# A's wo loaded and multiplied between two units of block B; the last V in one piece, B's wo straight behind it

## The chip, the core and the metric

The kernel runs on one core of one Trainium2 chip. The metric is the device time of one execution in microseconds (us); three executions of the kernel before took 1935.48, 1935.49 and 1935.57 us, median 1935.49 us. The engines named below are PE (TensorE, matrix products), DVE (VectorE), ACT (ScalarE), POOL (GpSimd) and SP (SyncE, which here only waits and issues DMAs).

## The reference, cut to what matters

Two independent attention blocks, A and B, each decode one token for a batch of 2 with 32 heads of 192 elements against a cache of 8192 positions. The outputs (2 x 1 x 640 each) are put side by side.

```python
q = (x @ wq)                                  # x 2x1x640, wq 640x6144, as 32 heads of 192
scores = einsum("bhqd,bhkd->bhqk", q, k) * (192 ** -0.5)
p = softmax(scores, axis=-1)
o = einsum("bhqk,bhkd->bhqd", p, v)           # k, v: 2x32x8192x192 bf16
return o.reshape(2, 1, 6144) @ wo             # wo 6144x640
```

The K and V caches of the two blocks make up nearly all of the 836.78 MB that the kernel reads.

## The kernel before, in words

A **unit** is a pair of heads of one batch row. Each block has 32 units (UB), so there are 64 (NP): 0 to 31 are A's, 32 to 63 are B's. For each unit a whole K piece and a whole V piece (6144 KB each) are loaded into a buffer in SBUF, `rings`, which has three slots of 7680 KB. In slots counted modulo 3, V of unit u goes into the slot where K of unit u lay, and K of unit u+1 goes into the slot where V of unit u-2 lay. A slot also holds a whole `wq` or `wo` (7680 KB).

What one unit does:
- DVE multiplies K in place by the query, in four quarters (L241). Each quarter releases `mu`.
- PE sums the products in groups with an identity matrix (L370), 12 matmuls a quarter, 48 in all; `su` counts the halves. When a unit's second half is done, its K slot is free.
- PE next places the result of an earlier unit into a bank of PSUM (`put`, L327, which waits for `on` of DVE), then sums the softmax denominators (L379, which waits for `ex` and `vs`), and then multiplies the **previous** unit's probabilities with its V: 4 groups of 16 matmuls (L385). Each group counts in `pv`.
- DVE reduces the scores (L246, L250, L251), POOL takes the maximum over partitions (L191), ACT copies the result of the V product out (`gather`, L286) and only then makes the unit's exponentials (L302), whose end is `ex`.

PE runs its units in a loop with index t: at t it does the scores of unit t and the V product of unit t-1. The loop body stands once in the code (`pe_main`) and is entered twice. The first time it runs t = 0 to 63, and behind it PE multiplies A's heads with A's wo (`rows`, L339, 96 matmuls). The second time it runs t = 64 (V product of unit 63) and t = 65 (the last `put`), and behind it PE multiplies with B's wo.

SP issues the loads in a fixed order: K of u+1, V of u, K of u+2, V of u+1 and so on, each behind its waits. The K load waits until K of unit u has landed (`ks`) and V of u-2 has been used (`pv`); the V load until V of u-1 has landed (`vs`) and K of u has been used (`su`). So at least one transfer is queued while another lands. Behind V of unit 62 come A's wo (L144, waits for V of unit 61 to be used), V of unit 63 in two halves (L150, waits for K of unit 63 to be used), and five pieces of B's wo (L155, 24, 15, 6, 2 and 1 rows), each of which waits in `ca` until PE has multiplied the same piece of A's wo, for it takes that place.

ACT copies the two products with wo out of PSUM (L312) and ACT and SP store them (L162). The output of `rows` lies in the PSUM bank `qps`, which the queries use as well.

Of the kernel before, what the change touches and what calls it, by code (L numbers as in the profile page):

```python
# [10 lines left out]
def build_kernel(nc, blocks, out):  # L11
    NBLK = len(blocks)
    B, Hn, Sk, Dh = blocks[0]["k"].shape
    D = blocks[0]["x"].shape[2]
# [3 lines left out]
    UB = B * PB  # L18
# [14 lines left out]
    PW = 34  # L33
    PG = 16
    PQ = T // 2 // PG
    CUTS = [48]
    PIECES = [24, 15, 6, 2, 1]

    with ExitStack() as es:
# [29 lines left out]
        ops = ps("ops", [128, 512], F32)  # L69
        qps = ps("qps", [128, 512], F32)  # L70
        oall = ps("oall", [128, 2, 512], F32)
        outps = qps
        scflat = scps[:].rearrange("p k n -> p (k n)")
        oflat = oall[:].rearrange("p k n -> p (k n)")

        Z = {n: sem(n) for n in ("held", "wq", "wq0", "wq1", "xs", "k0", "ks", "vs", "vh", "os", "init", "dv", "xp", "xt",
                                 "pr", "qe", "qk", "qtd", "mu", "su", "re", "mx", "ar", "nbd", "ex", "pv", "od", "dd", "on",
                                 "pl", "oa", "ca", "oe", "wa0")}
        vq = [sem(f"vq{i}") for i in range(2)]
        ws = [sem(f"ws{i}") for i in range(len(PIECES))]  # L80

        def hold(eng, name, value):
# [4 lines left out]
            return blocks[blk][name].rearrange("b h s d -> (b h s d)").rearrange("(u f) -> u f", f=RW)  # L87

        def k_slot(eng, t):
            return eng.snap(((t * 2 + 2 - ((t + (NP - 1)) >> 6)) % 3) * SW)  # L90

        def program_sync(eng):
            for blk in range(NBLK):
                w = blocks[blk]["wq"].rearrange("(j c) n -> j (c n)", c=DC)
                for a, e in (((0, N // 4), (N // 4, SW)) if not blk else ((0, SW),)):
                    eng.dma_start(rings[:, blk * SW + a:blk * SW + e], w[:, a:e]).then_inc(Z[f"wq{blk}"], 16)

            def load(name, blk, row, at, sem):
                src = flat(name, blk)
                src = src[row:row + 128, :] if isinstance(row, int) else src[bass.ds(row, 128), :]  # L100
                dst = rings[:, at:at + RW] if isinstance(at, int) else rings[:, bass.ds(at, RW)]
                eng.dma_start(dst, src).then_inc(Z[sem], 16)  # L102

            load("k", 0, 0, 2 * SW, "k0")
            eng.wait_ge(Z["pr"], NQP)
            load("k", 0, 128, 0, "ks")
            eng.wait_ge(Z["pr"], 2 * NQP)
            load("v", 0, 0, SW, "vs")
            eng.wait_ge(Z["su"], 2)

            def next_k(u, row, blk, at, wait_k, wait_p):
                hold(eng, "ks", wait_k)
                hold(eng, "pv", wait_p)
                load("k", blk, row, at, "ks")

            def next_v(u, row, blk, at, wait_v, wait_s):
                hold(eng, "vs", wait_v)
                hold(eng, "su", wait_s)
                load("v", blk, row, at, "vs")

            def step(t, u0, blk_v, blk_k):
                if isinstance(t, int):
                    u = u0
                    next_k(u, (u + 1) % UB * 128, blk_k, ((2 * u + 3) % 3) * SW, 16 * u + 16, PQ * (u + 1))
                    next_v(u, u % UB * 128, blk_v, ((2 * u + 4) % 3) * SW, 16 * u, 2 * u + 2)
                else:
                    u = eng.snap(t + u0)
                    r = eng.snap((u * 2) % 3)
                    rk, rv = eng.snap(t * 128 + (u0 + 1) % UB * 128), eng.snap(t * 128 + u0 % UB * 128)
                    next_k(u, rk, blk_k, eng.snap(r * SW), eng.snap(u * 16 + 16), eng.snap(u * PQ + PQ))  # L130
                    next_v(u, rv, blk_v, eng.snap(((r + 1) % 3) * SW), eng.snap(u * 16), eng.snap(u * 2 + 2))

            with eng.Fori(0, UB - 2) as t:
                step(t, 1, 0, 0)
            step(0, UB - 1, 0, 1)
            with eng.Fori(0, UB - 1) as t:
                step(t, UB, 1, 1)
            eng.wait_ge(Z["pv"], PQ * NP)
            for blk in range(NBLK):
                w = blocks[blk]["wo"].rearrange("(p r) n -> p (r n)", r=WR)  # L140
                if not blk:
                    r0 = 0
                    for k, n in enumerate(CUTS):
                        eng.dma_start(rings[:, r0 * D:(r0 + n) * D], w[:, r0 * D:(r0 + n) * D]).then_inc(Z[f"wa{k}"], 16)  # L144
                        r0 += n
                    eng.wait_ge(Z["su"], 2 * NP)
                    src = flat("v", 1)[(UB - 1) * 128:UB * 128, :]
                    for g in range(2):
                        a, e = g * RW // 2, (g + 1) * RW // 2
                        eng.dma_start(rings[:, SW + a:SW + e], src[:, a:e]).then_inc(vq[g], 16)  # L150
                else:
                    r0 = 0
                    for k, n in enumerate(PIECES):
                        eng.wait_ge(Z["ca"], k + 1)
                        eng.dma_start(rings[:, r0 * D:(r0 + n) * D], w[:, r0 * D:(r0 + n) * D]).then_inc(ws[k], 16)  # L155
                        r0 += n
            for blk in range(NBLK):
                eng.wait_ge(Z["oe"], blk + 1)
                store(eng, blk, 1)
# [5 lines left out]
        def program_pool(eng):  # L165
# [20 lines left out]
            for blk in range(NBLK):  # L186
                eng.wait_ge(Z[f"wq{blk}"], 32 - 16 * blk)
                eng.sem_inc(Z["wq"], 1)  # L188
            with eng.Fori(0, NP) as t:
                hold(eng, "mx", eng.snap(t + 1))  # L190
                eng.partition_all_reduce(mg[:], mp[:], 128, bass.bass_isa.ReduceOp.max).then_inc(Z["ar"], 1)  # L191
            k = 0
            for i, n in enumerate(CUTS):
                eng.wait_ge(Z[f"wa{i}"], 16)
                while k < len(PIECES) and sum(PIECES[:k + 1]) <= sum(CUTS[:i + 1]):
                    eng.sem_inc(ws[k], 16)
                    k += 1
            eng.wait_ge(vq[0], 16)
            eng.sem_inc(Z["vs"], 16)
            eng.wait_ge(vq[1], 16)  # L200
            eng.sem_inc(Z["vh"], 2)

        def spread(eng, blk):
            eng.wait_ge(Z["pl"], (blk + 1) * UB + 3)
# [6 lines left out]
        def program_vector(eng):  # L211
# [18 lines left out]

            eng.wait_ge(Z["k0"], 16)
            eng.sem_inc(Z["ks"], 16)
            with eng.Fori(0, NP) as t:
                u = eng.snap(t + 1)
                at = k_slot(eng, t)
                q3 = qt[:].unsqueeze(1).broadcast_to([128, TQ, Dh])
# [12 lines left out]
                eng.wait_ge(Z["re"], eng.snap(u * 2))  # L249
                eng.tensor_reduce(mp[0:64, 0:1], sc[0:64, :], AXL.X, ALU.max)  # L250
                eng.tensor_reduce(mp[64:128, 1:2], sc[64:128, :], AXL.X, ALU.max).then_inc(Z["mx"], 1)  # L251
            eng.wait_ge(Z["qtd"], NP + 2)
            spread(eng, 0).then_inc(Z["oa"], 1)
            closing(NP + 1)
            closing(NP + 2)

        def program_scalar(eng):
            eng.sem_inc(Z["qe"], 2)
            eng.sem_inc(Z["ex"], 2)
            eng.sem_inc(Z["od"], 1)  # L260
            eng.sem_inc(Z["qtd"], 1)
            eng.memzero(actd[:, 0:1]).then_inc(Z["xt"], 1)
            eng.wait_ge(Z["xt"], 1)
            eng.activation(actd[:, 1:2], actd[:, 0:1], ACTF.Exp)
# [51 lines left out]
        def program_tensor(eng):  # L316
# [15 lines left out]
            def rows(r0, r1, landed):  # L332
                at = 0
                for k, n in enumerate(PIECES):
                    for r in range(max(at, r0), min(at + n, r1)):
                        if r == at:
                            eng.wait_ge(ws[k], landed)
                        for h in range(2):
                            ins = eng.matmul(outps[32 * h:32 * h + B, 0:NH2], oallS[:, r, :],  # L339
                                             rings[:, r * D + h * NH2:r * D + (h + 1) * NH2],  # L340
                                             start=(r == 0), stop=(r == WR - 1))
                        if r == at + n - 1:
                            ins.then_inc(Z["ca"], 1)
                    at += n
# [7 lines left out]
            with nc.body("pe_main", valid_engines=own):  # L352
                loc = eng.mark_branch_hint_location()
                p = nc.snap(turn, min_val=0, max_val=NBLK - 1)
                late = eng.snap(p * 2)
                with eng.Fori(eng.snap(p * NP), eng.snap(p * 2 + NP)) as t:
                    w = eng.snap(t + 2)
                    with eng.If(t < NP):
                        eng.wait_ge(Z["qtd"], w)
# [12 lines left out]
                    with eng.If(t > 0):  # L372
# [3 lines left out]
                        with eng.If(t < NP + 1):  # L376
                            eng.wait_ge(Z["ex"], w)
                            eng.wait_ge(Z["vs"], eng.snap(t * 16))
                            eng.matmul(ops[0:PW, 448:449], rs[:], ones[:], start=True, stop=True)  # L379
                            v_at = eng.snap(((t * 2 + 2) % 3) * SW)  # L380
                            with eng.Fori(0, PQ) as g:
                                eng.wait_ge(Z["vh"], eng.snap((g & late) + 1))
                                aj, vj = eng.snap(g * (PG * PW)), eng.snap(g * (PG * 2 * Dh) + v_at)
                                for j in range(PG):
                                    ins = eng.matmul(ops[0:PW, 0:2 * Dh], pbflat[:, bass.ds(aj + j * PW, PW)],  # L385
# [1 line left out]
                                                     skip_group_check=True)  # L387
                                ins.then_inc(Z["pv"], 1)
                eng.wait_ge(Z["oa"], eng.snap(p + 1))
                landed = eng.snap(p * 16 + 16)  # L390
                rows(0, 6, landed)
                eng.br("pe_rows")
            with nc.body("pe_first", valid_engines=own):
                eng.sem_inc(Z["pl"], 2)
                eng.sem_inc(Z["pv"], 2 * PQ)
                eng.sem_inc(Z["vh"], 1)
                eng.wait_ge(Z["init"], INIT)
                eng.wait_ge(Z["xs"], 32)
                with eng.Fori(0, DC) as c:
# [81 lines left out]
```

## Time and profile before

| what | number |
|---|---|
| median of the runs | 1935.49 us |
| span of the profiled execution | 1934.3 us |
| bytes read from HBM, over the span | 836.77 MB, 433 GB/s |
| busy: PE, DVE, ACT, POOL | 81%, 56%, 10%, 1% |
| V products, L385, 4096 matmuls | 712.9 us busy |
| sums of K products, L370, 3072 matmuls | 749.0 us busy |
| K products, DVE L241, 256 | 842.5 us busy |

The span runs from the first to the last instruction of the profiled execution; no other time of that execution is given, and the median of the runs is 1.2 us above its span. Shares of busy time are averages over the whole span. Which engine sets the end can only be read at the end, and which sets the pace only in the middle: so the views of single stretches matter more than this table.

### The profile page before, as it was taken

The numbers are of one execution on the slowest core, as the hardware profiler recorded it, in microseconds if no ns is written. First come the engines' busy times: TensorE is split into PE (matmuls) and PEld (weight loads), VectorE is DVE, ScalarE is ACT, GpSimd is POOL, SyncE is SP. The second block draws the span as 40 slices with busy tenths as digits, with TensorE's granted clock in tenths as the row PEclk, the third lists the DMA queues.
The fourth block names the chain that finished last, engine by engine and source line by source line (L and its number), as shares of the span: only waits on it lengthen the run. The fifth ranks groups of instructions, "written<-read, shape, count | busy, mean of one in ns | idle before, by whom it ended". The sixth has DMA issues, their size and how long they took to land.

```text
span 1934.3 us, 31141 instructions
## 1 busy us (share of the span) xinstructions
PE 1558.2 (81%) x7939; PEld 743.0 (38%) x7939; DVE 1075.6 (56%) x717; ACT 186.5 (10%) x598; POOL 27.9 (1%) x83
## 2 busy tenths in 40 slices
PE   5787888887888887888887888887888888888887
PEld 1343333333333333333333333333433333433434
DVE  0665565565565565565565565565565565565560
ACT  2110010010010010010010010010010010010010
POOL 1000000000000000000000000000000000000000
PEclk9899999999999999999999999999999999999999
DMA  9999999999999999999999999999999999999999
GB/s 421 425 439 439 423 439 439 425 437 439 430 432 439 431 431 439 433 429 439 435 427 439 437 425 439 437 425 439 437 425 439 439 425 437 439 430 432 439 435 394
DMA packets 19896, 836.78 MB, mean 433 GB/s; under 512 B 2220, under 2 KB 2360, under 8 KB 2744
## 3 DMA queue, kind: packets, MB, share of 16 engines
q1 hardware_dynamic: 19880, 836.78, 100.0%
q10 hardware_dynamic: 16, 0.01, 0.0%
HBM read 836.77 MB, written 0.01 MB: 433 GB/s over the span
## 4 chain that ended last, share of the span: by engine, by line
DMA 44%; PE 32%; DVE 10%; issue 10%; another core or an unknown queue 2%; DVEq 1%; SPq 0%; ACT 0%; POOLq 0%
DMA rings<-in_B_k_cache_dram 22%; DMA rings<-in_A_k_cache_dram 19%; PE ops L385 18%; PE scps L370 12%; DVE rings L241 10%; DMA rings<-in_A_wo_dram 2%; DMA rings<-in_B_wo_dram 1%; DVEq L241 1%; PE oall L327 0%; PE qps L339 0%; PE ops L379 0%; SPq L102 0%; DVE qrow L212 0%; DVE sc L246 0%
## 5 line engine op out<-in xcount | busy, mean ns | idle before, releaser
L241 DVE TENSOR_TENSOR rings<-rings,qt 128x6144 bf16 x256 | 842.5, 3353 | 722.9 <-DMA rings<-in_B_k_cache_dram 351.0
L385 PE MATMUL ops<-rings,pb 128*34 x4096 | 712.9, 327 | 166.9 <-issue 166.9
L370 PE MATMUL scps<-rings,ident 128*128 x3072 | 749.0, 403 | 105.5 <-DVE rings L241 102.6
L385 PEld LDWEIGHTS ops<-rings,pb 128*34 x4096 | 381.3, 93 | 483.0 <-issue 233.5
L370 PEld LDWEIGHTS scps<-rings,ident 128*128 128x128 bf16 x3072 | 314.5, 102 | 524.0 <-issue 249.6
L246 DVE TENSOR_REDUCE sc<-scps 128x64 f32<-128x1024 f32 x128 | 155.5, 1215 | 81.4 <-PE scps L370 81.4
L286 ACT ACTIVATE oodd<-ops 2x192 f32<-2x192 f32 x65 | 20.9, 321 | 731.4 <-PE ops L385 731.4
L272 ACT ACTIVATE qt<-qps 64x192 bf16<-64x192 f32 x65 | 21.0, 323 | 650.1 <-DVE rings L241 649.6
L302 ACT ACTIVATE pb<-sc,nb 64x128 bf16<-64x128 f32 x128 | 82.4, 644 | 2.6
L322 PE MATMUL qps<-qrow,sel 36*128 (+1 forms) x66 | 21.8, 331 | 72.4 <-issue 69.6
L296 ACT ACTIVATE nb<-mg 64x1 f32<-64x1 f32 x128 | 25.7, 201 | 302.8 <-POOL mg L191 302.1
L191 POOL PARTITION_ALL_REDUCE mg<-mp x64 | 22.7, 354 | 1856.8 <-DVE mp L251 1856.8
L322 PEld LDWEIGHTS qps<-qrow,sel 36*128 (+1 forms) x66 | 6.1, 93 | 94.0 <-issue 94.0
L302 ACT ACTIVATION_READ_ACCUMULATOR pb<-sc,nb 64x1 f32 x128 | 39.2, 306 | 0.0
L411 PE MATMUL scps<-rings,xT 128*4 x120 | 29.4, 410 | 6.3 <-POOLq L188 6.3
L224 DVE RECIPROCAL rc<-ops 2x1 f32<-2x1 f32 x66 | 9.8, 149 | 34.5 <-PE ops L385 34.5
L327 PEld LDWEIGHTS oall<-on,place 2*128 x260 | 12.5, 92 | 29.7 <-issue 29.2
L226 DVE TENSOR_TENSOR oodd<-ops,oodd 2x192 f32<-2x192 f32 x66 | 21.5, 326 | 0.4 <-ACT oodd L286 0.4
L229 DVE TENSOR_SCALAR on<-oodd,rc 2x192 bf16<-2x192 f32 x66 | 20.3, 307 | 2.3
L273 ACT ACTIVATE qt<-qps 64x192 bf16<-64x192 f32 x65 | 21.1, 325 | 0.8
L327 PE MATMUL oall<-on,place 2*128 2x48 bf16 x260 | 19.6, 183 | 1.9 <-DVE on L229 1.7
L411 PEld LDWEIGHTS scps<-rings,xT 128*4 128x4 bf16 x120 | 10.7, 89 | 24.2 <-issue 12.2
(38 smaller groups left out, 109.9 us busy)
## 6 DMA issues: line engine op xcount, KB each, us to landing
rings<-in_A_k_cache_dram SPq DMA_DIRECT2D x32, 6144.0 KB, 26.8
rings<-in_A_v_cache_dram SPq DMA_DIRECT2D x32, 6144.0 KB, 26.5
rings<-in_B_k_cache_dram SPq DMA_DIRECT2D x32, 6144.0 KB, 26.7
rings<-in_B_v_cache_dram SPq DMA_DIRECT2D x31, 6144.0 KB, 26.6
rings<-in_B_wq_dram SPq DMA_DIRECT2D x1, 7680.0 KB, 37.9
rings<-in_A_wo_dram SPq DMA_DIRECT2D x1, 7680.0 KB, 30.7
rings<-in_A_wq_dram SPq DMA_DIRECT2D x1, 7296.0 KB, 20.2
rings<-in_B_v_cache_dram SPq DMA_DIRECT2D x2, 3072.0 KB, 26.8
```

The lines of the kernel that those rows point to most:

```text
L191: eng.partition_all_reduce(mg[:], mp[:], 128, bass.bass_isa.ReduceOp.max).then_inc(Z["ar"], 1)
L226: eng.tensor_tensor(oodd[:], ops[0:2, 0:Dh], oodd[:], ALU.add).then_inc(Z["dd"], 1)
L241: eng.tensor_tensor(k3, k3, q3, ALU.mult).then_inc(Z["mu"], 1)
L246: eng.tensor_reduce(sc[:, h * 2 * TQ:(h + 1) * 2 * TQ], scps[:, 2 * h:2 * h + 2, :].rearrange("p k (t g) -> p (k t) g", g=DG), AXL.X, ALU. ...
L273: eng.activation(qt[64:128, :], qps[64:128, Dh:2 * Dh], ACTF.Identity).then_inc(Z["qtd"], 1)
L296: ins = eng.activation(nb[p0:p0 + 64, :], mg[p0:p0 + 64, h:h + 1], ACTF.Identity, scale=-scale)
L302: ins = eng.activation(pb[p0:p0 + 64, :, h::32], sc[p0:p0 + 64, :].rearrange("p (j a) -> p j a", a=2), ACTF.Exp, bias=nb[p0:p0 + 64, :], s ...
L322: eng.matmul(qps[:, 0:2 * Dh], sel[:].rearrange("p s m -> p (s m)")[:, bass.ds(k, 128)], qrow[:, bass.ds(c, 2 * Dh)], start=True, stop=Tru ...
L327: ins = eng.matmul(oflat[:, bass.ds(sec, WR)], place[:, bass.ds(at - a, 128)], on[:, a * WR:(a + 1) * WR], start=False, stop=False, skip_g ...
L370: ins = eng.matmul(dst, ident[:], src[:, :, 0:DG], start=(j == 0), stop=(j == NJ - 1))
L385: ins = eng.matmul(ops[0:PW, 0:2 * Dh], pbflat[:, bass.ds(aj + j * PW, PW)], rings[:, bass.ds(vj + j * (2 * Dh), 2 * Dh)], start=False, st ...
L411: ins = eng.matmul(scflat[0:4, bass.ds(to + h * QC, QC)], xT[:, c, :], rings[:, bass.ds(at + (c * N + h * QC), QC)], start=(c == 0), stop= ...
```

## The change

A's wo is loaded between two units of block B. A new constant MID = 45 names the place: behind K of unit 46 and V of unit 45, SP issues A's wo into slot 2 (WO), where V of unit 44 lay. From there on every K and V lies one slot further on, which the new terms with TA = 47 in `k_slot` and in the V address say. PE's loop runs t = 0 to 46 on its first entry; behind it come A's rows, and on the second entry t = 47 to 65. DVE copies A's result out (`spread`) behind its unit 44, for which its loop is split in two.

At the end, V of unit 63 is loaded in one piece as soon as V of unit 61 has been used, and B's wo directly behind it into slot 2, with no wait between its pieces. The wait per V group on `vh`, with its two register operations, is gone from the V product. The product with wo now goes to the second bank of `oall` in place of `qps`.

SP's queue at the end of the program before (rows that issue a DMA, with the semaphores that they wait for; `pv` counts V products, `su` K sums, `ca` pieces of A's wo that have been used):

```order
L144 DMA rings<-in_A_wo_dram 128x30720 [waits pv]
L150 DMA rings<-in_B_v_cache_dram 128x12288 [waits su]
L150 DMA rings<-in_B_v_cache_dram 128x12288
L155 DMA rings<-in_B_wo_dram 128x15360 [waits ca]
L155 DMA rings<-in_B_wo_dram 128x9600 [waits ca]
L155 DMA rings<-in_B_wo_dram 128x3840 [waits ca]
L155 DMA rings<-in_B_wo_dram 128x1280 [waits ca]
L155 DMA rings<-in_B_wo_dram 128x640 [waits ca]
```

The same queue of the changed program, from the end of B's first loop on:

```order
L138 COMPARE_AND_BRANCH
L142 DMA rings<-in_A_wo_dram 128x30720 [waits pv]
L103 DMA rings<-in_B_k_cache_dram 128x24576 [waits ks,su]
L103 DMA rings<-in_B_v_cache_dram 128x24576 [waits vs,pv]
L103 DMA rings<-in_B_k_cache_dram 128x24576 [waits ks,ca]
L103 DMA rings<-in_B_v_cache_dram 128x24576 [waits vs,su]
L157 UNCONDITIONAL_BRANCH
```

And its end:

```order
L103 DMA rings<-in_B_v_cache_dram 128x24576 [waits pv]
L164 DMA rings<-in_B_wo_dram 128x15360 [waits su]
L164 DMA rings<-in_B_wo_dram 128x9600
L164 DMA rings<-in_B_wo_dram 128x3840
L164 DMA rings<-in_B_wo_dram 128x1280
L164 DMA rings<-in_B_wo_dram 128x640
```

A's wo has left the place between the last two V loads, and stands ahead of K of unit 47; the next four loads have their K and V waits exchanged, since their slots have moved on by one.

On PE, the start of one group of the V product before (register rows are marked ISA or REGISTER_ALU):

```order
L379 MATMUL ops<-ones,rs 34x1 [waits vs]
L381 UNCONDITIONAL_BRANCH
L381 ISA
L382 REGISTER_ALU x2
L385 ISA [waits vh]
L385 ISA
L385 MATMUL ops<-rings,pb 34x384
```

and the same place of the changed program:

```order
L391 MATMUL ops<-ones,rs 34x1 [waits vs]
L393 UNCONDITIONAL_BRANCH
L393 ISA
L396 ISA x2
L396 MATMUL ops<-rings,pb 34x384
```

Two register operations and a wait have left the loop over the four groups.

```diff
-    CUTS = [48]
+    MID = 45
+    TA = MID + 2
+    WO = 2 * SW
...
-        outps = qps
+        outps = oall[:, 1, :]
...
-            return eng.snap(((t * 2 + 2 - ((t + (NP - 1)) >> 6)) % 3) * SW)
+            return eng.snap(((t * 2 + 2 - ((t + (NP - 1)) >> 6) + ((t + (NP - TA)) >> 6)) % 3) * SW)
...
-            with eng.Fori(0, UB - 1) as t:
-                step(t, UB, 1, 1)
+            with eng.Fori(0, MID + 1 - UB) as t:
+                step(t, UB, 1, 1, 0)
+            eng.wait_ge(Z["pv"], PQ * (MID + 2))
+            eng.dma_start(rings[:, WO:WO + SW], wo[0]).then_inc(Z["wa0"], 16)
+            m = MID + 1
+            hold(eng, "ks", 16 * m + 16)
+            hold(eng, "su", 2 * m + 2)
+            load("k", 1, (m + 1) % UB * 128, ((2 * m + 4) % 3) * SW, "ks")
+            hold(eng, "vs", 16 * m)
+            hold(eng, "pv", PQ * (m + 2))
+            load("v", 1, m % UB * 128, ((2 * m + 5) % 3) * SW, "vs")
+            m = MID + 2
+            hold(eng, "ks", 16 * m + 16)
+            eng.wait_ge(Z["ca"], len(PIECES))
+            load("k", 1, (m + 1) % UB * 128, ((2 * m + 4) % 3) * SW, "ks")
...
+            with eng.Fori(0, NP - 1 - (MID + 3)) as t:
+                step(t, MID + 3, 1, 1, 1)
             eng.wait_ge(Z["pv"], PQ * NP)
...
-                        eng.dma_start(rings[:, r0 * D:(r0 + n) * D], w[:, r0 * D:(r0 + n) * D]).then_inc(Z[f"wa{k}"], 16)
...
-                        eng.dma_start(rings[:, SW + a:SW + e], src[:, a:e]).then_inc(vq[g], 16)
...
-                        eng.wait_ge(Z["ca"], k + 1)
-                        eng.dma_start(rings[:, r0 * D:(r0 + n) * D], w[:, r0 * D:(r0 + n) * D]).then_inc(ws[k], 16)
+            load("v", 1, (UB - 1) * 128, ((2 * NP - 1) % 3) * SW, "vl")
+            eng.wait_ge(Z["su"], 2 * NP)
...
+                eng.dma_start(rings[:, WO + r0 * D:WO + (r0 + n) * D], wo[1][:, r0 * D:(r0 + n) * D]).then_inc(ws[k], 16)
...
-            with eng.Fori(0, NP) as t:
+            def unit(t):
...
-            eng.wait_ge(Z["qtd"], NP + 2)
+            with eng.Fori(0, TA - 2) as t:
+                unit(t)
             spread(eng, 0).then_inc(Z["oa"], 1)
+            with eng.Fori(TA - 2, NP) as t:
+                unit(t)
...
-                late = eng.snap(p * 2)
-                with eng.Fori(eng.snap(p * NP), eng.snap(p * 2 + NP)) as t:
+                with eng.Fori(eng.snap(p * TA), eng.snap(p * (NP + 2 - TA) + TA)) as t:
...
-                            v_at = eng.snap(((t * 2 + 2) % 3) * SW)
+                            v_at = eng.snap(((t * 2 + 2 + ((t + (NP - TA)) >> 6) - (t >> 6)) % 3) * SW)
                             with eng.Fori(0, PQ) as g:
-                                eng.wait_ge(Z["vh"], eng.snap((g & late) + 1))
...
                 eng.wait_ge(Z["oa"], eng.snap(p + 1))
-                landed = eng.snap(p * 16 + 16)
+                eng.wait_ge(Z["wa0"], 16)
+                landed = eng.snap(p * 16 + 1)
                 rows(0, 6, landed)
```

More of the change, by code (lines that the diff above doesn't have):

```diff
@@ L71, in build_kernel @@
         oall = ps("oall", [128, 2, 512], F32)
-        outps = qps
+        outps = oall[:, 1, :]
         scflat = scps[:].rearrange("p k n -> p (k n)")
         oflat = oall[:].rearrange("p k n -> p (k n)")
-        Z = {n: sem(n) for n in ("held", "wq", "wq0", "wq1", "xs", "k0", "ks", "vs", "vh", "os", "init", "dv", "xp", "xt",
+        Z = {n: sem(n) for n in ("held", "wq", "wq0", "wq1", "xs", "k0", "ks", "vs", "vl", "os", "init", "dv", "xp", "xt",
                                  "pr", "qe", "qk", "qtd", "mu", "su", "re", "mx", "ar", "nbd", "ex", "pv", "od", "dd", "on",
                                  "pl", "oa", "ca", "oe", "wa0")}
-        vq = [sem(f"vq{i}") for i in range(2)]
         ws = [sem(f"ws{i}") for i in range(len(PIECES))]
@@ L119, in next_v, with step @@
                 load("v", blk, row, at, "vs")
-            def step(t, u0, blk_v, blk_k):
+            def step(t, u0, blk_v, blk_k, shift):
                 if isinstance(t, int):
                     u = u0
-                    next_k(u, (u + 1) % UB * 128, blk_k, ((2 * u + 3) % 3) * SW, 16 * u + 16, PQ * (u + 1))
-                    next_v(u, u % UB * 128, blk_v, ((2 * u + 4) % 3) * SW, 16 * u, 2 * u + 2)
+                    next_k(u, (u + 1) % UB * 128, blk_k, ((2 * u + 3 + shift) % 3) * SW, 16 * u + 16, PQ * (u + 1))
+                    next_v(u, u % UB * 128, blk_v, ((2 * u + 4 + shift) % 3) * SW, 16 * u, 2 * u + 2)
                 else:
                     u = eng.snap(t + u0)
-                    r = eng.snap((u * 2) % 3)
+                    r = eng.snap((u * 2 + shift) % 3)
                     rk, rv = eng.snap(t * 128 + (u0 + 1) % UB * 128), eng.snap(t * 128 + u0 % UB * 128)
@@ L131, in step @@
                     next_v(u, rv, blk_v, eng.snap(((r + 1) % 3) * SW), eng.snap(u * 16), eng.snap(u * 2 + 2))
+            wo = [blocks[blk]["wo"].rearrange("(p r) n -> p (r n)", r=WR) for blk in range(NBLK)]
             with eng.Fori(0, UB - 2) as t:
-                step(t, 1, 0, 0)
-            step(0, UB - 1, 0, 1)
-            with eng.Fori(0, UB - 1) as t:
-                step(t, UB, 1, 1)
-            eng.wait_ge(Z["pv"], PQ * NP)
[L139 to L153, printed above, removed]
-                        eng.wait_ge(Z["ca"], k + 1)
-                        eng.dma_start(rings[:, r0 * D:(r0 + n) * D], w[:, r0 * D:(r0 + n) * D]).then_inc(ws[k], 16)
-                        r0 += n
@@ new lines, in program_sync @@
+                step(t, 1, 0, 0, 0)
+            step(0, UB - 1, 0, 1, 0)
+            with eng.Fori(0, MID + 1 - UB) as t:
+                step(t, UB, 1, 1, 0)
+            assert (2 * MID + 2) % 3 == 2
+            eng.wait_ge(Z["pv"], PQ * (MID + 2))
[4 more added lines that the diff above has]
+            load("k", 1, (m + 1) % UB * 128, ((2 * m + 4) % 3) * SW, "ks")
@@ new lines, in program_sync @@
+            hold(eng, "vs", 16 * m)
[5 more added lines that the diff above has]
+            load("k", 1, (m + 1) % UB * 128, ((2 * m + 4) % 3) * SW, "ks")
+            hold(eng, "vs", 16 * m)
+            hold(eng, "su", 2 * m + 2)
+            load("v", 1, m % UB * 128, ((2 * m + 5) % 3) * SW, "vs")
+            with eng.Fori(0, NP - 1 - (MID + 3)) as t:
+                step(t, MID + 3, 1, 1, 1)
@@ L157, in program_sync @@
+            eng.wait_ge(Z["pv"], PQ * NP)
+            load("v", 1, (UB - 1) * 128, ((2 * NP - 1) % 3) * SW, "vl")
+            eng.wait_ge(Z["su"], 2 * NP)
+            r0 = 0
+            for k, n in enumerate(PIECES):
+                eng.dma_start(rings[:, WO + r0 * D:WO + (r0 + n) * D], wo[1][:, r0 * D:(r0 + n) * D]).then_inc(ws[k], 16)
+                r0 += n
             for blk in range(NBLK):
@@ L188, in program_pool, with maxima @@
                 eng.sem_inc(Z["wq"], 1)
-            with eng.Fori(0, NP) as t:
[L190 to L198, printed above, removed]
+            def maxima(a, e):
+                with eng.Fori(a, e) as t:
+                    hold(eng, "mx", eng.snap(t + 1))
+                    eng.partition_all_reduce(mg[:], mp[:], 128, bass.bass_isa.ReduceOp.max).then_inc(Z["ar"], 1)
+            for k in range(len(PIECES)):
+                eng.sem_inc(ws[k], 1)
+            maxima(0, NP)
+            eng.wait_ge(Z["vs"], 16 * (NP - 1))
+            eng.wait_ge(Z["vl"], 16)
             eng.sem_inc(Z["vs"], 16)
-            eng.wait_ge(vq[1], 16)
-            eng.sem_inc(Z["vh"], 2)
         def spread(eng, blk):
@@ L232, in program_vector @@
             eng.sem_inc(Z["ks"], 16)
-            with eng.Fori(0, NP) as t:
+            def unit(t):
                 u = eng.snap(t + 1)
@@ L261, in program_scalar @@
             eng.sem_inc(Z["qtd"], 1)
+            eng.sem_inc(Z["pl"], 2)
+            eng.sem_inc(Z["pv"], 2 * PQ)
             eng.memzero(actd[:, 0:1]).then_inc(Z["xt"], 1)
@@ L339, in rows @@
                             ins = eng.matmul(outps[32 * h:32 * h + B, 0:NH2], oallS[:, r, :],
-                                             rings[:, r * D + h * NH2:r * D + (h + 1) * NH2],
+                                             rings[:, WO + r * D + h * NH2:WO + r * D + (h + 1) * NH2],
                                              start=(r == 0), stop=(r == WR - 1))
@@ L393, in program_tensor @@
             with nc.body("pe_first", valid_engines=own):
-                eng.sem_inc(Z["pl"], 2)
-                eng.sem_inc(Z["pv"], 2 * PQ)
-                eng.sem_inc(Z["vh"], 1)
                 eng.wait_ge(Z["init"], INIT)
```

## The prediction

> **What bounds the kernel now.** I start with the page's DMA part and the windows, then SP's waits, then the last 70 us of the timeline. First the page, and the bytes in a long stretch of the middle (columns of a windows row: length; busy time of each engine with its instructions; granted clock; DMA share; GB/s).
>
> ```profile
> span 1934.3 us, 31141 instructions
> q1 hardware_dynamic: 19880, 836.78, 100.0%
> 200.00:1600.00 1400.00, 1136.82 (x5755) 544.21 (x5753) 803.99 (x532) 128.23 (x434) 17.35 (x49) 0.97 1.00 434
> 1866.70:1932.10 65.40, 52.28 (x395) 27.13 (x393) 18.60 (x18) 5.28 (x17) 0.35 (x1) 0.97 0.98 421
> SPq L84 <- DMA rings<-in_B_v_cache_dram: 357.4, 30, 12.0
> SPq L84 <- DMA rings<-in_B_k_cache_dram: 351.8, 31, 11.7
> ```
>
> In the middle the DMA engines are busy all the time at 434 GB/s. The two SP rows say why: after issuing a load, SP waits some 12 us (357.4/30, 351.8/31) for the **earlier** transfer to land. Every load is thus queued about 12 us before its turn, and the queue never runs dry. 836.78 MB at 434 GB/s take 1928 us of the 1934.3: before, transfers set the pace. Now the end, from the timeline (start, length, engine, line, operation, count, idle time before it):
>
> ```profile
> 1838.10 13.17 DVE L241 TENSOR_TENSOR rings<-rings,qt 128x6144 bf16 x4 [10.90 <-DMA rings<-in_B_k_cache_dram]
> 1867.12 13.16 DVE L241 TENSOR_TENSOR rings<-rings,qt 128x6144 bf16 x4 [11.05 <-DMA rings<-in_B_k_cache_dram]
> 1868.53 0.36 SPq L144 DMA_DIRECT2D rings<-in_A_wo_dram  x1
> 1877.64 5.58 PE L370 MATMUL scps<-rings,ident 128*128 x24 [0.95 <-DVE rings L241]
> 1883.25 0.83 SPq L150 DMA_DIRECT2D rings<-in_B_v_cache_dram  x2
> 1884.34 2.81 PE L385 MATMUL ops<-rings,pb 128*34 x16 [0.57 <-issue]
> 1894.79 2.77 PE L385 MATMUL ops<-rings,pb 128*34 x16 [0.71 <-issue]
> 1898.93 0.30 ACT L302 ACTIVATION_READ_ACCUMULATOR pb<-sc,nb 64x1 f32 x1
> 1899.37 6.68 PE L339 MATMUL qps<-rings,oallS 128*2 128x320 bf16 x96 [1.81 <-POOLq L196]
> 1902.83 4.14 SPq L155 DMA_DIRECT2D rings<-in_B_wo_dram  x5
> 1906.91 0.22 PE L379 MATMUL ops<-ones,rs 128*34 128x1 f32 x2
> 1907.75 2.77 PE L385 MATMUL ops<-rings,pb 128*34 x16 [0.62 <-issue]
> 1918.15 2.77 PE L385 MATMUL ops<-rings,pb 128*34 x16 [0.69 <-issue]
> 1923.73 4.69 PEld L339 LDWEIGHTS qps<-rings,oallS 128*2 128x2 bf16 x48 [0.65 <-issue]
> 1932.15 0.08 PEld L339 LDWEIGHTS qps<-rings,oallS 128*2 128x2 bf16 x2 [0.30 <-DMA rings<-in_B_wo_dram]
> ```
>
> The last K (unit 63) lands just ahead of 1867.12. PE's chain from there is: K sums to 1883.22 (DVE's quarters pace it), V product of unit 62 to 1897.56, A's rows, V product of unit 63 to 1920.92, B's rows. A's rows start 0.1 us after A's wo landed, as the chain of waits shows, and the last matmuls wait for B's wo:
>
> ```profile
> 1868.53 30.75 DMA rings<-in_A_wo_dram
> 1905.68 25.22 DMA rings<-in_B_wo_dram
> 1930.95 1.52 PE qps L339 x18
> ```
>
> So the end is a DMA end too. Had B's wo been there, its 96 matmuls, begun at 1923.73, would have been done about 1 us earlier (7.8 us, below, gives 1931.5 against 1930.95 + 1.52 = 1932.47). **PE has about 1 us of slack here**, and only because A's wo (18 us of transfer) stands between the last two V loads. That slack decides this change.
>
> **The transfers.** No byte is added or removed, so the question is whether the queue stays full and what is left to compute once the last K has landed. Two K starts lie 1867.12 - 1838.10 = 29.0 us apart for two loads of 6144 KB, 14.5 us each; A's wo, 7680 KB, takes 14.5 x 7680/6144 = 18.1 us. The bytes between two V loads move ahead of K of unit 47: **the last K lands 18.1 us later**, at about 1885 in the old count.
>
> The middle, counted from DVE's start on K of unit 46 (0) with the old offsets: V 44 is used at 1868.53 - 1867.12 = 1.4, so A's wo is issued there. V 45 lands at 14.1, A's wo at 32.2. K 46 is used at 16.1 (1883.22), so K 47 is issued 16 us ahead of its turn. V 45 is used at 30.4 (1897.56), then V 46 is issued, also 16 us ahead of 46.7, when K 47 lands. A's rows run from about 32.5 to 39.2 (6.68 us); PE would otherwise idle until K 47, so they cost nothing there. Their `ca` frees K 48, which waits for K 47 to land (46.7) anyway; its turn comes at 61.2. The in-order SP holds up nothing with these waits: each is met 12 us or more ahead of an empty queue. Without this cover each microsecond of a dry queue would cost one. The two extra loop entries (DVE, SP, PE) fall into idle times of 11 us (DVE's row above), 12 us and 7 us. I price the middle at 0; below, nothing can be gained by a queue that is already full; above, a late K 48 would have to be 22 us late (61.2 - 39.2) to count.
>
> **The end.** Now V 63 is issued 1.4 after DVE's start on the last K and lands at 14.1 + 14.5 = 28.6, ahead of its use. B's wo follows and lands at 46.7, that is at 1867.12 + 18.1 + 46.7 = 1931.9, as before: the bytes are the same. But PE's chain does not get its 18.1 us back. Step by step, in the old count plus 18.1:
> - V product of unit 62 ends at 1897.56 + 18.1 = 1915.66.
> - Before, A's rows covered ACT's exponentials of unit 63 (done at 1898.93 + 0.30 = 1899.23, 1.67 behind the V product). Now PE waits for them, and needs 0.84 from L379 to the first matmul (1907.75 - 1906.91): 2.55 with the step between. 1918.21.
> - V product of unit 63: 1907.75 to 1920.92, 13.17. 1931.38.
> - Copy, `put` and spread up to B's rows: 1923.73 - 1920.92 = 2.81. 1934.19. B's wo is complete by then.
> - B's rows, all 96 in one go. The rows for their speed (matmuls in brackets, granted clock third from the end):
>
> ```profile
> 1900.00:1902.00 2.00, 2.00 (x34) 1.27 (x31) 0.00 (x0) 0.00 (x0) 0.00 (x0) 1.00 0.91 393
> 1924.00:1926.00 2.00, 2.00 (x18) 0.99 (x16) 0.00 (x0) 0.00 (x0) 0.00 (x0) 0.50 1.07 461
> 1926.00:1928.00 2.00, 2.00 (x26) 1.10 (x22) 0.00 (x0) 0.00 (x0) 0.00 (x0) 0.74 0.85 365
> ```
>
> At the full clock A's 96 took 6.68 us. B's met a clock of 0.50 after the pause ahead of them: their first 48 loads took 4.69, and 48 at 34 in 2 us take 2.8, with 0.3 for the last to end: 7.8. I take 7.8, since the same pause stands there again. Low end 6.68; high end, at 18 in 2 us throughout, 10.7. 1941.99.
> - Copy out and store: 1934.3 - 1932.47 = 1.83. 1943.82.
>
> The V product's loop has lost two register operations and a wait per group. PE's queue at a group's start, 1861.1 to 1862.6 (ns; first and last start):
>
> ```profile
> L381 PEldq COMPARE_BRANCH  x1: 227/227/227, 1861.3 to 1861.3; - x1
> L382 PEldq ALU_OP  x2: 42/42/43, 1861.7 to 1861.8; - x2
> L385 PEldq FUSED_REGOPS  x4: 69/74/178, 1861.9 to 1862.5; - x4
> ```
>
> The two operations start at 1861.7 and 1861.8, the next at 1861.9: 0.1 each with their spacing, in a gap of about 0.7 us where PE waits for its queue. They are worth up to 0.2 a group, 0.3 with the wait, but the V address has more terms now (no row shows their price; the fused row of 178 ns, which the address is part of, is the nearest). I take 0.125 a group; 4 groups in two V products make 1.0 us, ends 0 and 2.4. In the middle this saves nothing, since PE waits there for K.
>
> **Sum:** 1943.82 - 1.0 = 1942.8 of span against 1934.3, that is +8.5 us; on the median, 1.2 above the span, **1944.0 us, +0.44%**. The "ca" waits and the halves of V 63 go at no gain: the five pieces were issued at 1902.83, some 11 us ahead of V 63's landing (1884.8 + 29 = 1913.8), and behind the change V 63 is whole before PE asks for it.
>
> **The clock.** The pause ahead of B's rows is 2.81 us with a `put` in it, and behind it the granted clock was 0.50 (row of 1924). [...]
>
> **The rivals.**
> 1. *No clock drop ahead of B's rows.* Of the pauses shown, that at 1899 (1.81 us) had none. Then rows take 6.68 and the time is 1944.0 - 1.1 = **1942.9 us**. [...]
> 2. *A clock drop in the V product of unit 63 too.* Its pause of 2.55 us is new. From 0.50 at 1924 to 0.74 at 1926 the clock is low for some 3.4 us; at half pace that loses up to 1.7: **1945.7 us**.
> 3. *A's wo slips in partly.* The page's GB/s in 40 slices:
>
> ```profile
> GB/s 421 425 439 439 423 439 439 425 437 439 430 432 439 431 431 439 433 429 439 435 427 439 437 425 439 437 425 439 437 425 439 439 425 437 439 430 432 439 435 394
> ```
>
> The best slices reach 439 against the mean of 434. Were that a queue that is not quite full, a unit would have 0.33 us to spare (29.0 x 5/439), 18 units behind the change 6 us: **1938 us**. The DMA share of 1.00 in the middle speaks against it. (The 394 of the last slice is mostly the 2 us behind the last landing, and not a queue run dry.)
> 4. *The other side: faster.* If most of A's wo went through in transfer time that is idle today, the last K would not move, and B's wo would land at 1931.9 less the same gain: PE's chain from the old K start gives 1942.8 - 18.1 = 1924.7 of span, **1926 us**. It turns faster than before once more than 8.5 of the 18.1 us are hidden in the middle. Against it stands SP's 12 us of waiting for an earlier transfer.
> 5. *The middle runs dry*, by a wait met late (K 48 behind `ca`, say): every microsecond beyond 22 us of cover counts; 5 us would give **1949 us**.
> 6. *The change does not do what it says* (A's wo stays where it was): the order of SP's queue excludes it.
>
> **Chances.** Forecast (one drop, ahead of B's rows) 0.45, rival 1 0.23, rival 2 0.17, rival 3 0.05, rival 4 0.03, rival 5 or a PE end slower still 0.07. The range takes in the first three with their unknown prices: low end 1942.9 with the loop's saving at its 2.4 (another 1.4 off), 1941.5; high end 1945.7 with no saving and somewhat slower rows, 1947.5. A measurement of this kernel can tell some 0.2% (3.9 us) from no change: slower 0.92, same 0.05, faster 0.03.
>
> **What the profile after should show.** A's wo issued in the middle of B; behind it DVE's K starts once 47 us apart and then 29.0 again; GB/s in those slices as ever; DVE's last K start near 1885; V product of unit 63 about 2.5 us behind that of unit 62; B's wo landed near 1932, ahead of the start of B's rows near 1933; no DMA wait in B's rows. The forecast is wrong if the last K starts well ahead of 1885 (transfers were not full), if some gap in the DMA row opens behind A's wo, or if the two V products at the end are much shorter than 13 us.

## The result, and the profile after

The changed kernel took 1947.72 us (median of four runs, 1946.68 to 1948.02) beside 1935.53 us of the kernel before (1935.48 to 1936.09). The ratio is 1.0061, with a 95% interval of 1.0047 to 1.0075: slower by 0.6%. Two later rounds of the same kernel on other occasions gave 1947.41 us (ratio 1.0054, 1.0038 to 1.0071) and 1946.10 us (1.0052, 1.0035 to 1.0068). The forecast was 1944.0 us, 8.5 us more than before, with a range up to 1947.5. The direction and the mechanism hold. The measured change of 12.2 us is larger than the forecast one, and this median lies 0.2 us above the range; the section on the prediction takes the terms apart, one of which varies from run to run.

The page and two windows of the changed kernel:

```profile
span 1946.5 us, 30606 instructions
q1 hardware_dynamic: 19736, 836.77, 99.3%
200.00:1600.00 1400.00, 1131.03 (x5770) 542.42 (x5769) 792.34 (x524) 127.31 (x430) 17.11 (x48) 0.96 1.00 434
1932.00:1934.00 2.00, 0.31 (x3) 0.09 (x1) 0.81 (x3) 0.32 (x1) 0.00 (x0) 1.00 0.01 3
```

The middle, which holds A's wo now, runs at the same 434 GB/s with the DMA engines busy all the time. But at 1932 the transfers are over, 14 us ahead of the end of the span. Before, they ended about 2 us ahead of it (PE's last weight loads of B's rows, which waited for B's wo, start at 1932.15 of 1934.3).

Around the place where A's wo is loaded, the timeline of the changed kernel (start, length, engine, line):

```profile
1374.34 3.36 DVE L249 TENSOR_TENSOR rings<-rings,qt 128x6144 bf16 x1 [10.84 <-DMA rings<-in_B_k_cache_dram]
1375.77 0.36 SPq L142 DMA_DIRECT2D rings<-in_A_wo_dram  x1
1390.55 0.36 SPq L103 DMA_DIRECT2D rings<-in_B_k_cache_dram  x1
1404.86 0.34 SPq L103 DMA_DIRECT2D rings<-in_B_v_cache_dram  x1
1406.61 6.68 PE L352 MATMUL oall<-rings,oallS 128*2 128x320 bf16 x96 [1.86 <-DMA rings<-in_A_wo_dram]
1420.95 0.34 SPq L103 DMA_DIRECT2D rings<-in_B_k_cache_dram  x1
1421.46 6.63 DVE L249 TENSOR_TENSOR rings<-rings,qt 128x6144 bf16 x2 [29.14 <-DMA rings<-in_B_k_cache_dram]
1450.48 3.36 DVE L249 TENSOR_TENSOR rings<-rings,qt 128x6144 bf16 x1 [10.80 <-DMA rings<-in_B_k_cache_dram]
```

Once, two K starts lie 1421.46 - 1374.34 = 47.1 us apart, and the next two 29.0 again: A's wo costs its 18.1 us of transfer and nothing besides. Its 96 matmuls lie at 1406.61, in the idle time of PE ahead of K of unit 47. (Of the four loads behind A's wo only the first two, K of unit 47 and V of unit 46, have their waits exchanged, other than the section on the change says; K of unit 48 waits for A's rows, and V of unit 47 waits as ever.)

The end, from the chain of waits (start, length, what):

```profile
1885.46 3.37 DVE rings L249
1889.51 12.22 PE scps L382 x48
1902.65 2.77 PE ops L396 x16
...
1913.04 2.84 PE ops L396 x16
1915.90 0.33 ACT oodd L299
1916.26 0.36 DVE oodd L234
1916.64 0.32 DVE on L237
1916.95 0.54 issue
1917.50 0.63 PE oall L340 x4
1918.19 0.22 PE ops L391 x2
1918.98 2.79 PE ops L396 x16
...
1929.43 2.79 PE ops L396 x16
1933.90 0.61 PE oall L340 x4
1935.12 9.63 PE oall L352 x96
1944.78 0.43 ACT out_sb L325
```

There is no DMA in it any more from the last K to the end. It is DVE and PE on the last K, the V products of units 62 and 63, and B's rows. Before, the last wait of this chain was for a transfer of B's wo.

### The profile page after: what moved, and what is told of

It reads as the page before. It is cut to its first block, busy times and chain, and to the rows that moved or that the text cites. A ratio compares the mean times of both kernels' runs of the same rounds, so it can differ in the third digit from the quotient of the medians.

```text
span 1946.5 us, 30606 instructions
## 1 busy us (share of the span) xinstructions
PE 1559.7 (80%) x7939; PEld 744.1 (38%) x7939; DVE 1075.6 (55%) x717; ACT 186.8 (10%) x598; POOL 28.0 (1%) x83
## 4 chain that ended last, share of the span: by engine, by line
DMA 42%; PE 36%; DVE 9%; issue 9%; another core or an unknown queue 2%; DVEq 1%; SPq 0%; ACT 0%
DMA rings<-in_B_k_cache_dram 23%; DMA rings<-in_A_k_cache_dram 19%; PE ops L396 19%; PE scps L382 15%; DVE rings L249 9%; DVEq L249 1%; PE oall L352 0%; PE oall L340 0%; PE ops L391 0%; SPq L103 0%; DVE qrow L220 0%; DVE sc L254 0%; DVE oall L224 0%; DVEq L231 0%
```

## The experiments

Times are medians; "span" is the span of the instructions in each run's record. Short diffs are against the changed kernel, or, where it says so, against the kernel before.

**A0, A1. The changed kernel again**, as a yardstick.

> The changed kernel once more, as the yardstick of the runs beside it. Theory 1 (the end is PE's chain behind the last K): 1946.7 to 1948.0 us as before, more spread than the kernel before, because the granted clock in B's rows varies from run to run.

> The changed kernel beside it: spans of 1943.6 to 1946.5 us, as its runs had so far, times of 1945 to 1948 us.

Measured 1947.41 us and 1946.10 us; the eight spans lie between 1943.6 and 1945.3 us. The kernel before, in the same rounds, has spans of 1934.1 to 1934.6 us. The changed kernel spreads more than three times as wide, as theory 1 expects of an end that hangs on PE. One run of A0 took 1945.07 us, below the 1946.7 that were expected at the least.

**E1. A's wo twelve units later.**

```diff
-    MID = 45
+    MID = 57
```

> A's wo 12 units later (behind K of unit 58). Theory 1 (A's wo takes its 18 us of transfer wherever it stands ahead of the last K; the middle costs nothing of its own): as the changed kernel, within 1 us. Rival (the units behind the move are slower, by their new slots and addresses): the loss of 12 us shrinks with the units behind it from 17 to 5, to about 3.6 us, that is 8 us faster than the changed kernel.

Measured 1946.20 us (ratio 1.0054, 1.0037 to 1.0071), beside 1947.41 us for A0. The difference of 1.2 us is 0.2 more than was expected, but within the spread (spans 1943.7 to 1945.5, beside 1943.6 to 1945.3), and far from the 8 us of the rival. In this kernel's profile the V product of unit 62 starts at 1902.71, in that of the changed kernel at 1902.65. Between these two places of A's wo there is no difference; the units behind the move are not slower.

**E2. The kernel before without A's wo load** (A's output is computed from other data).

```diff
-                        eng.dma_start(rings[:, r0 * D:(r0 + n) * D], w[:, r0 * D:(r0 + n) * D]).then_inc(Z[f"wa{k}"], 16)
...
-                eng.wait_ge(Z[f"wa{i}"], 16)
```

> The kernel before without A's wo load: A's rows multiply what lies in the slot, and V of unit 63 is queued directly behind V of unit 62. Theory 1 (A's wo covered PE's work behind the last K): of 18 us of transfer taken away only 1 to 4 us come back, about 2.4 us faster, since PE's chain behind the last K stays. Rival (the end of the kernel before is the end of its transfers and nothing else is near): 14 to 18 us faster.

Measured 1932.03 us beside 1935.73 us (ratio 0.9984, 0.9974 to 0.9993): 3.7 us of the 18 come back. Two windows of this kernel show that the transfers even stand still (second number from the end: DMA share):

```profile
1881.00:1884.00 3.00, 2.71 (x17) 1.15 (x14) 1.82 (x2) 0.06 (x1) 0.00 (x0) 1.00 0.00 0
1899.00:1902.00 3.00, 3.00 (x48) 1.95 (x46) 0.00 (x0) 0.25 (x2) 0.00 (x0) 1.00 0.02 8
```

PE is busy there while the DMA engines wait for it: V of unit 63 for the last K sums and B's wo for A's rows, whose places they take. And in this kernel's chain of waits no transfer stands between the last K and the end. So behind the last K the kernel before was nearly as much bound by PE as by its transfers: A's wo filled time in which PE had work anyway. This is the same mechanism as in the changed kernel, without any of its new code.

**E3. The changed kernel without B's wo load** (B's output is computed from other data).

```diff
-                eng.dma_start(rings[:, WO + r0 * D:WO + (r0 + n) * D], wo[1][:, r0 * D:(r0 + n) * D]).then_inc(ws[k], 16)
...
-                landed = eng.snap(p * 16 + 1)
+                landed = 1
```

> B's wo is not loaded; B's rows multiply what lies in the slot. Theory 1: the end waits for no transfer, so nothing changes, within 1 us of the changed kernel (the clock in B's rows). Rival (the end is still the end of the transfers): 18 us less transfer, up to 18 us faster.

Measured 1946.34 us (ratio 1.0054, 1.0037 to 1.0070), spans 1943.6 to 1945.2, as A0 and A1. Eighteen microseconds of transfer at the very end are worth nothing: the end of the changed kernel waits for no transfer.

**E4. The kernel before without B's wo load**: the same edit there (B's output is computed from other data).

> The kernel before without B's wo load: B's rows multiply what lies in the slot. Theory 1: PE's chain has about 1 us of slack against the last transfer, so the time falls by about 1 us (2 us with a full clock in B's rows; 1 us slower with two low stretches). Rival (the last pieces of B's wo cost the end much more than the chain of PE): 5 us faster or more.

Measured 1935.22 us beside 1935.73 us (ratio 0.9995, 0.9986 to 1.0005). Three of the ten runs took 1933.3 to 1933.5 us, seven 1934.8 to 1935.6: between 2.4 and 0.1 us faster. This fits the length of B's rows: one of the seven was profiled, with rows of 8.04 us and a span of 1933.5, and with 6.68 us in their place (an estimate) the span would be 1932.1, as the three have it (1932.1 to 1932.3). The kernel before has a slack of this size against its last transfer, no more; and since its end waits for that transfer, its time hardly shows how fast B's rows are.

**E5. The kernel before with the last V in one piece.**

```diff
-                    for g in range(2):
-                        a, e = g * RW // 2, (g + 1) * RW // 2
-                        eng.dma_start(rings[:, SW + a:SW + e], src[:, a:e]).then_inc(vq[g], 16)
+                    eng.dma_start(rings[:, SW:SW + RW], src).then_inc(vq[0], 16)
...
-            eng.wait_ge(vq[1], 16)
```

> The kernel before with V of unit 63 in one piece. Theory 1: there, the V product waits for the whole V (landed at about 1913.7 in place of a first half that is there by 1907.7), PE's chain loses its 1 us of slack and more: 5 to 8 us slower. Rival (the halves do not matter): no change.

Measured 1942.13 us beside 1935.73 us (ratio 1.0033, 1.0021 to 1.0044): 6.4 us slower. The timeline of this kernel:

```profile
1913.93 0.27 PE L376 MATMUL ops<-ones,rs 128*34 128x1 f32 x2 [7.07 <-POOLq L197]
1914.75 9.86 PE L382 MATMUL ops<-rings,pb 128*34 x48 [0.54 <-issue]
```

PE stands idle for 7.07 us until the whole V is there. In the changed kernel the whole V is no loss: it is issued at 1886.95 and lands 27.4 us later, at 1914.3, before PE has finished unit 62; PE asks for it only at 1918.2. So of the parts of the change, "the last V whole" is dear where A's wo stands ahead of it, and free where it does not.

**E6, E8. PE's pause ahead of B's rows filled** with matmuls that nobody reads: nine of 36 rows in E6, six of all 128 rows in E8.

```diff
+                        with eng.If(t > NP):
+                            for _ in range(6):
+                                eng.matmul(scps[:, 0, :], ident[:], rings[:, 0:512], start=True, stop=True)
                         eng.wait_ge(Z["on"], w)
```

> Nine matmuls of 128x384 that nobody reads fill PE's pause between the last V product and the last put. Theory (B's 96 matmuls took 9.6 us because the clock was at 0.50 behind the pause): they take 6.7 us, the time falls by some 2 to 3 us. Rival (they are slow because the product goes to another bank of PSUM, or out of another slot): they stay at 9.6 us, and the time stays or rises by up to 1 us.

> As e6, but the matmuls that fill the pause use all 128 rows and columns of the array (six of 128x128 by 512) in place of 36 rows. If what counts for the clock is how much of the array works, the clock stays at 1.00 ahead of B's rows, which take 6.7 us in the profile, and the spans no longer spread over 3 us: all near 1944. If the pause itself (0.9 us ahead of the first of them) is enough, or the clock follows something else, B's rows take 8.0 us or more again in the profile or in some of the spans. The time outside the span, 5.0 us in e6 against 1.5 to 2.6, is looked at too: no theory.

E6 was a miss: 1949.99 us (ratio 1.0070, 1.0053 to 1.0086), with the clock at 0.50 in its profile all the same, and spans from 1944.0 to 1945.8. In E8's profile the clock stands at 1.00, and its four spans are 1944.1 to 1944.2 us. First E6, then E8 (granted clock third from the end, PE's matmuls in the first brackets), then B's rows of E1, which has no filling:

```profile
1936.00:1938.00 2.00, 2.00 (x18) 0.97 (x16) 0.00 (x0) 0.00 (x0) 0.00 (x0) 0.50 0.00 0
```

```profile
1935.58 6.87 PE L352 MATMUL oall<-rings,oallS 128*2 128x320 bf16 x96 [0.53 <-ACT oallS L215]
1936.00:1938.00 2.00, 2.00 (x34) 1.28 (x30) 0.00 (x0) 0.00 (x0) 0.00 (x0) 1.00 0.00 0
```

```profile
1935.19 6.68 PE L352 MATMUL oall<-rings,oallS 128*2 128x320 bf16 x96 [0.66 <-ACT oallS L215]
```

So the clock is what makes B's rows long, and neither the other bank of PSUM nor the other slot: E1's rows use both and take 6.68 us, as A's rows do there in the changed kernel. That the filling kept the clock in E8 is likely, not shown. E1's profile, and E9's below, have the full clock in B's rows without it, and nine of the 24 runs with this end in which no filling was executed (the first four, A0, A1, E1, E3 and E9) have spans of 1943.6 to 1944.3 too; what speaks for the filling is that all four spans of E8 are alike. It is no gain as a change, though: E8 took 1948.98 us (ratio 1.0068, 1.0051 to 1.0085), because 4.7 to 5.0 us of its time lie outside the span, where the changed kernel has 1.5 to 2.6.

**E9. The same matmuls in the program, never executed** (`t > NP + 1`).

> e8's code with a condition that never holds: the six matmuls stand in PE's program and are not executed. e6 and e8 took 4.7 to 5.1 us of device time outside the span of their instructions, the changed kernel 1.5 to 2.6. If that follows from PE's longer program, it is about 5 us here too; if it follows from executing the matmuls, it is 1.5 to 2.6 us, and the time is that of the changed kernel within 1 us.

Measured 1945.50 us (ratio 1.0053, 1.0036 to 1.0069), with 1.5 to 2.3 us outside the span; in its profile B's rows took 6.68 us. So the extra 3 us go with executing them, not with the longer program. Where they lie, no view shows; that stays open.

**E7. The changed kernel with the last K in two halves**, DVE starting on the first.

```diff
-            with eng.Fori(0, NP - 1 - (MID + 3)) as t:
+            with eng.Fori(0, NP - 2 - (MID + 3)) as t:
                 step(t, MID + 3, 1, 1, 1)
...
+            for g in range(2):
+                a, e = g * RW // 2, (g + 1) * RW // 2
+                eng.dma_start(rings[:, WO + a:WO + e], src[:, a:e]).then_inc(Z[f"kh{g}"], 16)
...
+                    if last and q % 2 == 0:
+                        eng.wait_ge(Z[f"kh{q // 2}"], 16)
```

> The changed kernel with K of unit 63 in two halves, DVE starting on the first 7 us earlier; the last unit of DVE's loop stands on its own. Theory 1 (the end is the chain DVE, PE behind the last K): DVE no longer sets the pace of the K sums, PE still has to end unit 61's V product first (1886.9): 1.5 to 3 us faster than the changed kernel. Rival (something else sets the end): no change.

Measured 1945.24 us (ratio 1.0047, 1.0030 to 1.0064), spans 1941.5 to 1943.3, beside 1943.6 to 1946.5 of all runs of the changed kernel. Its profile and that of A0 have B's rows of the same 8.36 us, and spans of 1943.3 and 1945.3: 2.0 us faster, as expected. The timeline of E7:

```profile
1878.14 6.63 DVE L261 TENSOR_TENSOR rings<-rings,qt 128x6144 bf16<-128x6144 bf16 x2 [3.56 <-DMA rings<-in_B_k_cache_dram]
1885.39 6.63 DVE L261 TENSOR_TENSOR rings<-rings,qt 128x6144 bf16<-128x6144 bf16 x2 [0.62 <-DMA rings<-in_B_k_cache_dram]
1888.96 12.21 PE L395 MATMUL scps<-rings,ident 128*128 x48 [0.63 <-DVE rings L261]
1901.38 5.51 PE L409 MATMUL ops<-rings,pb 128*34 x32
```

DVE is done 6.6 us earlier (1892.0), but PE starts its K sums only 0.55 us earlier, at 1888.96 against 1889.51, since it still has unit 61's V product ahead of it. The sums then take as long as before, 12.21 us against 12.22, though DVE was expected to hold them up no longer. The other 1.4 us come behind them: the first two groups of unit 62's V product follow at once and without a gap (1901.38, 32 matmuls), where the changed kernel begins at 1902.65 and pauses 0.68 us between them. In the changed kernel PE's queue works out the first addresses of these groups from 1902.2 on, 0.5 us behind the end of the sums (1901.73); in E7 PE had them in time for the first load at 1901.35. Why the queue was earlier is not shown; that DVE's products were done so early fits it. So a shorter chain ahead of the end does shorten the time, but the size was met in part by luck.

No version that computes both outputs beat the kernel before. That none of this kind can is argued, not shown: in those whose windows show it (the first run, A0, A1, E6 and E8) the bytes land near 1932, with a DMA share of 0.69 to 0.72 from 1930 to 1932 and of 0.00 to 0.01 in the next 2 us, and the kernel before ends about 2 us later.

## Why the prediction was right, point by point

1. *The queue stays full in the middle; A's wo costs 18.1 us there and nothing else.* Shown: 47.1 us between two K starts, 434 GB/s, and E1. The last K started at 1885.46, against 1867.12 + 18.1 = 1885.2.
2. *The end turns from a DMA end into a PE end.* Shown by the chain of waits, by E3 (no transfer is waited for) and by E2 (PE's work behind the last K was nearly binding before). The rivals in which A's wo slips into idle transfer time (3 and 4) and that of a dry queue (5) are out. Rivals 1 and 2 are about the clock; see below.
3. *The sum was short by 3.7 us of span* (1946.5 against 1942.8). Step by step: last K + 0.2; the loop's saving that did not come + 1.0; the step to the V product of unit 63 + 0.55; B's rows 9.63 in place of 7.8, + 1.8; the rest under 0.1. On top, the time outside the span, which I took as 1.2 us, was 1.5 us in the profiled execution and up to 2.4 in the other three. That the result lies near the top of the range is luck in part: of the range's 3.5 us above the forecast, 1.7 were the price of rival 2, which cost nothing, and the step to unit 63's V product, which did cost, was not in them.

The mis-sized term that counts is **B's rows**. I took one low stretch of the clock, as the profile of before showed, and put a longer one (10.7 us for the rows, at 18 matmuls in 2 us throughout) outside what I summed. Four profiles with this end have 6.68 us (E1), 8.02 (A1), 8.36 (A0) and 9.62 (the first run), and span less rows is 1937.0, 1936.9, 1936.9 and 1936.9. In these four profiles all spread is thus this one term; the other runs of these kernels have no profile. Other things can vary too: in E9's profile the rows took 6.68 us and the span less rows is 1937.6, since its chain is late already ahead of them: the last group of unit 63's V product starts at 1930.14, in the others at 1929.39 to 1929.49. In the first run, the windows show 0.50 twice in a row:

```profile
1934.00:1936.00 2.00, 1.37 (x12) 0.77 (x13) 0.00 (x0) 0.28 (x1) 0.00 (x0) 0.58 0.00 0
1936.00:1938.00 2.00, 2.00 (x18) 0.94 (x16) 0.00 (x0) 0.00 (x0) 0.00 (x0) 0.50 0.00 0
1938.00:1940.00 2.00, 2.00 (x18) 1.05 (x16) 0.00 (x0) 0.00 (x0) 0.00 (x0) 0.50 0.00 0
1940.00:1942.00 2.00, 2.00 (x26) 1.07 (x24) 0.00 (x0) 0.00 (x0) 0.00 (x0) 0.72 0.00 0
1942.00:1944.00 2.00, 2.00 (x34) 1.30 (x30) 0.00 (x0) 0.00 (x0) 0.00 (x0) 1.00 0.00 0
```

At 0.50 in the low stretch and 1.00 outside it, these rows make a low stretch of some 6.8 us (1.7 + 2 + 2 + 1.1), an estimate; the rows of A0 (0.90, 0.50 and 0.75 from 1934 to 1940) make 3.4. So the same pause ahead of the same rows was followed by no low stretch (E1, rows of 6.68 us), by one of some 3.4 us (A0, 8.36 us), or by one of some 6.8 us (the first run, 9.62 us). What sets its length is not shown.

So rival 1, no clock drop ahead of B's rows, came true in E1 and, by their spans, likely in A0's and A1's shortest runs; at 1943.6 to 1943.7 their spans still lie 1.9 us above the rival's 1941.7 (1942.9 less 1.2), for the terms on the chain ahead of the rows. The condition of **rival 2**, a clock drop in the V product of unit 63, was met in A0 and likely in E1, where 48 matmuls of this product run on without a gap (9.77 us from 1919.05), but its price of up to 1.7 us was wrong. A0:

```profile
1918.00:1920.00 2.00, 1.37 (x7) 0.74 (x8) 0.00 (x0) 0.05 (x1) 0.00 (x0) 0.63 1.10 476
1920.00:1922.00 2.00, 2.00 (x8) 0.98 (x7) 0.00 (x0) 0.00 (x0) 0.00 (x0) 0.51 0.73 317
1919.03 6.79 PE L396 MATMUL ops<-rings,pb 128*34 x32 [0.57 <-issue]
```

The product took 13.2 us from its first to its last matmul (1919.03 to 1932.27), as in the first run (1918.98 to 1932.22), where the clock stood at 1.00. The slower matmuls only filled the gaps between the groups: A0 has 32 matmuls in 6.79 us and a gap of 0.21, 7.00 together, and the first run 2.79 and 2.82 us with gaps of 0.69 and 0.71, 7.01 together.

**The loop's saving** was mis-read. Two operations and a wait left the loop over the V groups, yet the gap between groups stayed 0.66 to 0.71 us. PE's queue at a group's start, one row of the kernel before, then three of the changed kernel from 1883.0 to 1884.5 (ns):

```profile
L381 PEldq FUSED_REGOPS  x1: 41/41/41, 1861.6 to 1861.6; - x1
L393 PEldq COMPARE_BRANCH  x1: 223/223/223, 1883.2 to 1883.2; - x1
L393 PEldq FUSED_REGOPS  x1: 191/191/191, 1883.4 to 1883.4; - x1
L396 PEldq FUSED_REGOPS  x4: 56/76/253, 1883.7 to 1884.3; - x4
```

The operation behind the branch took 41 ns before and takes 191 now, and the longest of the address operations has gone from 178 to 253: 225 ns came where some 200 went. The longer slot formula, worked out anew in each group, is the likely cause; no run without it was made.

**The step to unit 63's V product** (3.10 us against 2.55): I let `put` run while ACT makes the exponentials. The chain shows it in series: `on` ends at 1916.95, PE begins `put` 0.54 us later and ends it at 1918.13, after `ex` (ACT's last row ends at 1917.55).

What I said of the halves of V holds (E5: 6.4 us where they matter, nothing in the changed kernel), and so does the slack of about 1 us (E4: 0.5 us at the median, 0.1 to 2.4).

## What to carry to other kernels

This kernel, bound by its transfers in the middle (434 GB/s, DMA share 1.00), ended after the change with the work that its last K brings with it (E3: no gain from 18 us less of transfer behind it). In such a case, order the last transfers so that those with the most work behind them come first and cheap ones fill the time behind them: here two weights of 18 us each, with 7 us of matmuls each, stood behind the last K in the kernel before. With one of them taken away to an earlier place, at no cost there but its transfer, PE's chain behind the last K is 59.3 us (1885.46 to 1944.75) and the transfers behind it end after 46.5 (at 1932). It cost 9 to 12 us of span (1943.6 to 1946.5 against 1934.3). Before moving a transfer out of the end, count PE's chain from the last large input to the end, and compare it with the bytes that are left behind that input.

## What was not expected of the hardware

- Filling a pause of PE with matmuls of 36 rows (1.62 us of them) did not keep the granted clock at 1.00 in the profile (0.50 at 1936), though two of the four spans (1944.0 and 1944.4) are as short as those with a full clock; with 1.46 us of 128 rows the clock was 1.00 in the profile, and all four spans lie within 0.1 us. Four runs each, and short spans without any filling, do not tell whether it counts how much of the array works; this stays open.
- B's rows, whose weights are 128x2, ran through some 6 us of a low stretch at 0.50 in one run (to about 1941.1, an estimate from the windows above) though PE was busy all the time from 1935.12.
- A clock of 0.50 for some 3 us in the V product of unit 63 cost no time (13.2 us with it and without), since it went into the gaps of 0.7 us between the groups (0.21 us of the second one left in A0).
- The device time outside the span of the instructions is no constant: 1.2 to 1.5 us in most runs of the kernel before, 1.5 to 2.6 in the changed kernel, 4.7 to 5.1 in E6 and E8. Its cause is open.
